# Float64 weight decode inside an attention and MLP kernel: one 4 KB row per partition and weight piece, the integer add on VectorE, words in a contiguous tile

## The chip, the core and the metric

The kernel runs on one core of a Trainium2 chip. The metric is device time in microseconds (us), the median of several executions. A core has a matrix engine (TensorE, PE in the profile; its weight loads are PEld), three elementwise engines (VectorE is DVE, ScalarE is ACT, GpSimd is POOL), and SyncE (SP), on whose queue all transfers of this kernel are issued. Each engine runs its own instructions in the order in which they stand; engines wait for each other on semaphores.

## The reference

Attention with a local window, a few global keys and a distance penalty, and behind it an MLP with GELU:

```python
scores = q @ k.T / 8                       # 4 batches, 8 heads, 768 tokens, head size 64
keep   = (col < n_global) | ((0 <= row - col) & (row - col < n_local))
dist   = n_local where only global, else abs(row - col)
a      = softmax(where(keep, scores - slope[h] * dist, -1e9))
x      = (a @ v)                           # 3072 tokens x 512
out    = gelu(x @ w_in) @ w_out            # w_in 512 x 2048, w_out 2048 x 512
```

`q`, `k` and `v` are float32. The two weight arrays arrive as float64, 8 MB each, and the kernel must make float32 numbers of them on the chip.

## The kernel before, in words

**The main loop.** The 3072 tokens are 12 chunks of 256, the 2048 columns of the hidden layer 8 slices of 256. Step T = 8 * chunk + slice, from 0 to 95, multiplies one chunk with one slice. `m1` (L457) makes the hidden values: 24 TensorE products named h (L468), 12 for each half of the slice, since each float32 operand is split in a high and a low part and three of the four products are taken. `gelu` (L472) applies GELU on ScalarE into gr (L478), makes its high part gh on GpSimd (L145) and its low part gl = gr - gh on VectorE (L148). `m2` (L483) multiplies gh and gl with the slice of `w_out` into acc (L495), 12 products. So TensorE needs gl of each step. gl0 is the low part of step 0, gl7 that of step 7: after it each slice has been used once. Steps -11 to -1 start the attention of chunks 0 and 1, whose scores and products run on float32 operands that are not split; its results go through xs (L422), a transpose (L452), xh (L454) and xl (L148) to become x. The attention of the later chunks is spread over the steps of the chunks before them (reductions n at L348, q at L277, k and others through L148).

**The weights.** A slice is four pieces of 512 KB, 128 partitions x 512 numbers x 8 bytes; I number them 4 * slice + i, from 0 to 31. Pieces i = 0 and 1 are 256 rows of `w_in` by the slice's 256 columns, which makes two runs of 2 KB per partition; i = 2 and 3 are 128 rows of `w_out`, 4 KB per partition. A piece lies in SBUF as pairs of 32-bit words, low and high word of a float64 side by side. The decode (L170 to L200) takes, per piece: on ScalarE, the low word times 2^-29, rounded to an integer, back into the low word's place (the scale, L184); on VectorE, 27 bits of the high word shifted by 3 (the mask, L186), into a contiguous tile `wb`; on GpSimd, the integer add of the two (the add, L188), into `wb`; on VectorE, that with the top two bits of the high word (the merge, L189), back into the high word's place, every second word; on ScalarE, a copy rounded to fp32r, the high part of the weight (the copy, L198); on VectorE, the difference, the low part (L200). fp32r is the float32 form that TensorE takes as a split operand. For pieces 12 and 26 GpSimd makes the high part instead, for piece 7 the low part (L42, L195, L199).

**Buffers.** Pieces of slices 0 to 6 rotate through five buffers (`ws`), those of slice 7 through the four of `stg`, which serve other loads too. A buffer is free again when its last reader is done: before, the low part of L200, since the finished float32 lies in it. Transfers of pieces are kept in order. From step 16 to 48 each piece is loaded once more, and three ScalarE operations check that its exponents lie in the range in which the short decode is right (`check_words`, L205); their scratch tile comes from `stg`.

**The order.** The program is written step by step: slice s is decoded at step `DECODE[s]` (L39: -4, -3, -2, -1, 0, 2, 2, 2), ahead of that step's other work. But the order in which instructions stand on each engine is not the written one: a scheduler arranges them by its own model of costs and by the dependencies, and it runs anew for the changed kernel.

Of the kernel before, what the change touches and what calls it, by code (L numbers as in the profile page):

```python
# [28 lines left out]
MAXLOCAL = 97.0  # L29
# chunks whose attention runs in native float32 products; the others split their operands  # L30
NATIVE = (0, 1)
# step at which a chunk's attention starts, and the steps after it at which its parts are issued
START = [-10, -5, 4] + [8 * c - 13 for c in range(3, NCH)]
# [3 lines left out]
       "pt": (2, 3, 4, 5), "av": (2, 3, 4, 5), "xt": (3, 4, 5, 6)}  # L37
# step at which a weight slice is decoded; slices from LATE on live where the native chunks' operands were
DECODE = (-4, -3, -2, -1, 0, 2, 2, 2)  # L39
LATE = 5  # L40
# work that GpSimd takes over from the other engines: weight halves (high, low part), V of a chunk
HI_POOL, LO_POOL, V_POOL = (12, 26), (7,), (2,)  # L42
NEGMASK = -1000000000.0
# [22 lines left out]
class Fast:  # L66
    def __init__(self, tc, ctx, qT, kT, v, w_in, w_out, out, limits):
        self.tc, self.nc = tc, tc.nc
        self.qT, self.kT, self.v, self.w_in, self.w_out, self.out = qT, kT, v, w_in, w_out, out
# [79 lines left out]

    def word_src(self, s, i):  # L150
        if i < 2:
            return self.w_in[i * 256:(i + 1) * 256, s * 512:(s + 1) * 512].rearrange("(d p) f -> p d f", p=P)
        r = s * 256 + (i - 2) * P
        return self.w_out[r:r + P, :].rearrange("p (d f) -> p d f", d=2)

    def load_words(self, s, i, use):
        pool, tag = (self.ws, "ws") if use == "w" and s < NST - 1 else (self.stg, "stage")
        w = pool.tile([P, 2, 256, 2], I32, name=f"{use}{s}_{i}", tag=tag)
        ins = self.nc.sync.dma_start(w.rearrange("p d f t -> p d (f t)"), self.word_src(s, i)).ins
# [10 lines left out]
    def split_weights(self, s):  # L170
# [9 lines left out]
        for i in range(4):  # L180
            w = self.raw.pop((s, i, "w"))
            lw, hw = w[:, :, :, 0], w[:, :, :, 1]
            a, t = hw, lw
            nc.scalar.activation(out=t, in_=lw.bitcast(U32), func=AF.Copy, scale=2.0 ** -29)  # L184
            bt = self.sm.tile([P, 2, 256], I32, name=f"wb{s}_{i}", tag="o")
            nc.vector.tensor_scalar(out=bt, in0=hw, scalar1=0x07FFFFFF, scalar2=3,  # L186
                                    op0=ALU.bitwise_and, op1=ALU.logical_shift_left)
            nc.gpsimd.tensor_tensor(out=bt, in0=bt, in1=t, op=ALU.add)  # L188
            nc.vector.scalar_tensor_tensor(out=a, in0=hw, scalar=-0x40000000, in1=bt,  # L189
                                           op0=ALU.bitwise_and, op1=ALU.bitwise_or)  # L190
            if i < 2:
                hi, lo = (x[:, 2 * i:2 * i + 2, :] for x in self.win[s])
            else:
                hi, lo = (x[:, i - 2, :].rearrange("p (d f) -> p d f", d=2) for x in self.wout[s])
            if s * 4 + i in HI_POOL:  # L195
                self.hi_pool(hi, a.bitcast(F32))
            else:
                nc.scalar.copy(hi, a.bitcast(F32))  # L198
            eng = nc.gpsimd if s * 4 + i in LO_POOL else nc.vector  # L199
            eng.tensor_tensor(out=lo, in0=a.bitcast(F32), in1=hi.bitcast(F32), op=ALU.subtract)  # L200

# [400 lines left out]
def round_words(nc, pool, out, src):  # L602
    n = out.shape[1]
# [3 lines left out]
    nc.sync.dma_start(w.rearrange("p f t -> p (f t)"), src)  # L607
    lw, hw = w[:, :, 0], w[:, :, 1]
# [29 lines left out]

def general(tc, qT, kT, v, w_in, w_out, out, limits):
    nc = tc.nc  # L640
    NB = S // P
    NF = DF // P
    with ExitStack() as ctx:
# [92 lines left out]

def body(tc, qT, kT, v, w_in, w_out, limits, out):
    nc = tc.nc
    w_in, w_out = w_in.bitcast(I32), w_out.bitcast(I32)
    with tc.tile_pool(name="flagp", bufs=1) as fp:  # L740
        flag_i = fp.tile([1, 1], I32, name="flag_i")
        with ExitStack() as ctx:
            fast = Fast(tc, ctx, qT, kT, v, w_in, w_out, out, limits)
            fast.run()
            fast.flag(flag_i)
        fv = nc.values_load(flag_i, min_val=0, max_val=1)
        with tc.If(fv):
            general(tc, qT, kT, v, w_in, w_out, out, limits)

# [21 lines left out]
```

## Time and profile before

| what | value |
|---|---|
| median of 3 runs | 737.23 us (736.77 to 737.34) |
| span of the profiled execution | 735.9 us |
| TensorE busy | 709.4 us, 96% of the span |
| VectorE, ScalarE, GpSimd busy | 481.6, 420.9, 349.4 us |
| mean granted TensorE clock | 0.994 |
| masks of the decode (L186), first and last start | 12.0 and 120.1 us |
| low part of step 0 and of step 7 (gl0, gl7), start | 71.35 and 127.82 us |

One execution was profiled, and all durations come from it. A row of a timeline is: start in us, duration in us, engine, line, operation, output<-inputs, size, and in square brackets how long the engine had been idle before and what ended that. A row of groups is: line, engine, operation and tiles, count, then busy us, mean ns of one, then idle us before them. The duration of one instruction holds its start-up and its tail, and consecutive ones overlap a little, so that the distance of two starts can be less than the duration of the first. A row with x2 in a timeline stands for two instructions in succession. Line numbers are those of the kernel before.

### The profile page before, as it was taken

Reading aid. Unit: us, or ns where it says so; the run is one execution under the profiler, and the core shown is the slowest. Engines: PE = TensorE matmul, PEld = TensorE weight load, DVE = VectorE, ACT = ScalarE, POOL = GpSimd, SP = SyncE. Lnnn points to the kernel's source line nnn. Section 1 sums busy time; section 2 is a strip of 40 time slices with the busy share of each in tenths; the row PEclk is TensorE's granted clock in tenths of the full one; section 3 lists DMA queues with packets and bytes.
Section 4 is the critical chain, followed back from the end, with each engine's and each line's share of the span. In section 5 each row is a group of like instructions: output and inputs, shape, how many; then the busy total and the mean of one; then the engine's idle time right before and its main releaser. Section 6 shows DMA issues by size and latency. Waiting matters only on the chain.

```text
span 735.9 us, 13621 instructions
## 1 busy us (share of the span) xinstructions
PE 709.4 (96%) x4617; PEld 642.8 (87%) x4617; DVE 481.6 (65%) x1219; ACT 420.9 (57%) x1032; POOL 349.4 (47%) x607
## 2 busy tenths in 40 slices
PE   6899878999999999999999999999999999999996
PEld 4778667899999999999999999999999999999995
DVE  6989999757846856746756757757657758643111
ACT  5658544555759769769669556355355455452101
POOL 4666666674445555543444545543444545431110
PEclk9999999999999999999999999999999999999999
DMA  8964563333526546535546513223213211100000
GB/s 264 263 191 143 175 213 81 117 83 101 146 78 171 166 123 177 158 108 158 160 125 174 153 44 87 72 62 94 76 47 109 83 29 44 45 15 1 29 1 33
DMA packets 78492, 80.92 MB, mean 110 GB/s; under 512 B 12368, under 2 KB 63056, under 8 KB 78416
## 3 DMA queue, kind: packets, MB, share of 16 engines
q1 hardware_dynamic: 78416, 79.98, 37.5%
q8 instruction: 38, 0.62, 0.4%
q14 instruction: 38, 0.31, 0.1%
HBM read 73.66 MB, written 6.29 MB: 109 GB/s over the span
## 4 chain that ended last, share of the span: by engine, by line
PE 85%; DVE 8%; DMA 2%; issue 1%; ACT 1%; SPq 1%; POOL 1%; POOLq 0%; DVEq 0%; ACTq 0%
PE h L468 35%; PE acc L495 33%; PE t L389 5%; PE s L343 5%; PE av L431 5%; DMA w<-w_in 2%; DVE winl L200 2%; DVE w L189 2%; PE s L339 2%; DVE woutl L200 1%; DVE wb L186 1%; PE av L417 1%; DVE gl L148 1%; ACT n L363 0%; DVE n L348 0%
## 5 line engine op out<-in xcount | busy, mean ns | idle before, releaser
L468 PE MATMUL h<-xh,winh 128*128 128x256 f32 x768 | 221.1, 289 | 1.5 <-ACT xh L454 1.4
L468 PE MATMUL h<-xh,winl 128*128 128x256 f32 x768 | 218.6, 285 | 0.4 <-DVE winl L200 0.4
L468 PE MATMUL h<-xl,winh 128*128 128x256 f32 x768 | 218.9, 285 | 0.0
L495 PE MATMUL acc<-wouth,gl 128*128 128x512 f32 x384 | 150.0, 399 | 7.2 <-DVE gl L148 7.2
L495 PE MATMUL acc<-wouth,gh 128*128 128x512 f32 x384 | 154.4, 402 | 0.9 <-POOL gh L145 0.9
L468 PEld LDWEIGHTS h<-xh,winh 128*128 128x128 f32 x768 | 146.9, 192 | 7.2 <-ACT xh L454 1.8
L495 PE MATMUL acc<-woutl,gh 128*128 128x512 f32 x384 | 152.4, 397 | 0.0
L468 PEld LDWEIGHTS h<-xl,winh 128*128 128x128 f32 x768 | 147.2, 192 | 3.7 <-issue 0.3
L148 DVE TENSOR_TENSOR gl<-gr,gh 128x512 fp32r<-128x512 f32 x96 | 68.2, 710 | 122.9 <-POOL gh L145 122.3
L468 PEld LDWEIGHTS h<-xh,winl 128*128 128x128 f32 x768 | 147.3, 192 | 0.8 <-DVE winl L200 0.6
L478 ACT ACTIVATE gr<-h 128x512 f32<-128x512 f32 x96 | 57.3, 597 | 82.9 <-PE h L468 75.0
L376 POOL TENSOR_SCALAR n<-n,su 128x256 f32<-128x256 f32 (+1 forms) x160 | 71.2, 466 | 55.2 <-DVE su L368 37.5
L145 POOL TENSOR_SCALAR gh<-gr 128x512 fp32r<-128x512 f32 x96 | 64.0, 667 | 69.6 <-ACT gr L478 69.6
L363 ACT ACTIVATE n<-n,mn 128x256 f32<-128x256 f32 (+1 forms) x192 | 91.8, 480 | 8.3 <-DVE mn L348 8.0
L145 POOL TENSOR_SCALAR vt<-vr 128x256 fp32r<-128x256 f32 (+1 forms) x80 | 34.1, 426 | 130.8 <-PE av L431 83.6
L495 PEld LDWEIGHTS acc<-wouth,gl 128*128 128x128 f32 x384 | 72.8, 190 | 24.4 <-DVE gl L148 9.0
L495 PEld LDWEIGHTS acc<-wouth,gh 128*128 128x128 f32 x384 | 73.2, 191 | 12.3 <-POOL gh L145 1.3
L495 PEld LDWEIGHTS acc<-woutl,gh 128*128 128x128 f32 x384 | 73.2, 190 | 11.8
L348 DVE CUSTOM_DVE_ANT_0 n<-s,pen 128x256 f32<-128x256 f32 (+1 forms) x192 | 69.3, 394 | 16.1 <-PE s L343 13.6
L396 ACT CAST pt<-t 128x512 fp32r<-128x512 f32 (+1 forms) x80 | 44.3, 553 | 60.6 <-PE t L389 56.2
L438 ACT COPY t<-av 64x256 f32<-64x256 f32 x80 | 29.3, 367 | 83.0 <-PE av L431 79.9
L188 POOL TENSOR_TENSOR wb<-wb,w 128x512 int32<-128x512 int32 x32 | 48.0, 1501 | 36.6 <-DVE wb L186 17.3
(92 smaller groups left out, 1158.2 us busy)
## 6 DMA issues: line engine op xcount, KB each, us to landing
kr<-kT SPq DMA_DIRECT2D x112, 112.0 KB, 2.8
qr<-qT SPq DMA_DIRECT2D x88, 128.0 KB, 2.9
w<-w_in SPq DMA_DIRECT2D x16, 512.0 KB, 4.7
w<-w_out SPq DMA_DIRECT2D x16, 512.0 KB, 4.5
c<-w_in SPq DMA_DIRECT2D x16, 512.0 KB, 4.2
c<-w_out SPq DMA_DIRECT2D x16, 512.0 KB, 4.4
vr<-v SPq DMA_DIRECT2D x48, 128.0 KB, 2.3
out<-o SPq DMA_DIRECT2D x24, 256.0 KB, 2.1
```

What stands on the lines that cost most here:

```text
L145: self.nc.gpsimd.tensor_scalar(out=out, in0=in_, scalar1=scale, scalar2=0.0, op0=ALU.mult, op1=ALU.add)
L148: self.nc.vector.tensor_tensor(out=out, in0=in_, in1=hi.bitcast(F32), op=ALU.subtract)
L188: nc.gpsimd.tensor_tensor(out=bt, in0=bt, in1=t, op=ALU.add)
L343: nc.tensor.matmul(sp[:, j, :w], lhsT=qq[:, hh, j * P:(j + 1) * P], rhs=kt[:, t, 0 if first else j, :w], start=t == 0, stop=t == 1)
L348: nc.vector.tensor_tensor_reduce(out=nn[:, j, :w], in0=sp[:, j, :w], in1=pen, scale=-slope(h), scalar=3e38, op0=ALU.add, op1=ALU.min, accu ...
L363: ins = nc.scalar.activation(out=nn[:, j, :w], in_=nn[:, j, :w], func=AF.Exp, bias=mn[:, i:i + 1], scale=-1.0, accum_out=su[:, i:i + 1])
L376: nc.gpsimd.tensor_scalar(out=nn[:, j, :w], in0=nn[:, j, :w], scalar1=su[:, i:i + 1], scalar2=0.0, op0=ALU.mult, op1=ALU.add)
L389: nc.tensor.transpose(tp[:, i, :], nn[:, j, a * P:(a + 1) * P], self.ident)
L396: nc.scalar.copy(pt[:, :, 0, :], tp[:, :n, :])
L468: nc.tensor.matmul(hp[:, f, :], lhsT=w[:, d, f * P:(f + 1) * P], rhs=x[:, d, :], start=n == 0, stop=n == 3 * NP - 1)
L478: self.table(nc.scalar.activation(out=gr, in_=hp, func=AF.Gelu))
L495: nc.tensor.matmul(acc, lhsT=g[:, f, ks], rhs=w[:, f, :], start=s == 0 and n == 0, stop=s == NST - 1 and n == 5)
```

## The change

All weights become one array of 32 pieces, [32, 128, 512] of 8-byte numbers, laid out on the host so that each piece is one 4 KB row per partition. So pieces 0 and 1 of a slice, too, are one run per partition instead of two; bytes and transfers are as many as before. In the decode the two steps on the words change places, and all of mask, merge and add work in the contiguous tile `a` (named wb), the add on VectorE instead of GpSimd. Then the copy and the low part read `a`, and the last reader of a piece's buffer is the add. `a` has two buffers, of the pool that `wb` had. No piece's high or low part goes to GpSimd any more. The check's scratch tile `cq` comes from that same pool instead of `stg`. The general version behind a flag (`general`, `round_words`), which does not run on these inputs, reads the new array.

```diff
-HI_POOL, LO_POOL, V_POOL = (12, 26), (7,), (2,)
+V_POOL = (2,)
...
     def load_words(self, s, i, use):
         pool, tag = (self.ws, "ws") if use == "w" and s < NST - 1 else (self.stg, "stage")
-        w = pool.tile([P, 2, 256, 2], I32, name=f"{use}{s}_{i}", tag=tag)
-        ins = self.nc.sync.dma_start(w.rearrange("p d f t -> p d (f t)"), self.word_src(s, i)).ins
+        w = pool.tile([P, 512, 2], I32, name=f"{use}{s}_{i}", tag=tag)
+        ins = self.nc.sync.dma_start(w.rearrange("p f t -> p (f t)"), self.w[s * 4 + i]).ins
...
             w = self.raw.pop((s, i, "w"))
-            lw, hw = w[:, :, :, 0], w[:, :, :, 1]
-            a, t = hw, lw
-            nc.scalar.activation(out=t, in_=lw.bitcast(U32), func=AF.Copy, scale=2.0 ** -29)
-            bt = self.sm.tile([P, 2, 256], I32, name=f"wb{s}_{i}", tag="o")
-            nc.vector.tensor_scalar(out=bt, in0=hw, scalar1=0x07FFFFFF, scalar2=3,
+            lw, hw = w[:, :, 0], w[:, :, 1]
+            nc.scalar.activation(out=lw, in_=lw.bitcast(U32), func=AF.Copy, scale=2.0 ** -29)
+            a = self.sm.tile([P, 512], I32, name=f"wb{s}_{i}", tag="o")
+            nc.vector.tensor_scalar(out=a, in0=hw, scalar1=0x07FFFFFF, scalar2=3,
                                     op0=ALU.bitwise_and, op1=ALU.logical_shift_left)
-            nc.gpsimd.tensor_tensor(out=bt, in0=bt, in1=t, op=ALU.add)
-            nc.vector.scalar_tensor_tensor(out=a, in0=hw, scalar=-0x40000000, in1=bt,
+            nc.vector.scalar_tensor_tensor(out=a, in0=hw, scalar=-0x40000000, in1=a,
                                            op0=ALU.bitwise_and, op1=ALU.bitwise_or)
+            nc.vector.tensor_tensor(out=a, in0=a, in1=lw, op=ALU.add)
+            af = a.bitcast(F32)
...
-            if s * 4 + i in HI_POOL:
-                self.hi_pool(hi, a.bitcast(F32))
-            else:
-                nc.scalar.copy(hi, a.bitcast(F32))
-            eng = nc.gpsimd if s * 4 + i in LO_POOL else nc.vector
-            eng.tensor_tensor(out=lo, in0=a.bitcast(F32), in1=hi.bitcast(F32), op=ALU.subtract)
+            nc.scalar.copy(hi, af)
+            self.lo_dve(lo, af, hi)
...
-        q = self.stg.tile([P, 2, 256], F32, name=f"cq{n}", tag="stage", padded_shape=[P, 4, 256])
-        nc.scalar.activation(out=q, in_=w[:, :, :, 1], func=AF.Square, scale=2.0 ** -27)
+        q = self.sm.tile([P, 512], F32, name=f"cq{n}", tag="o")
+        nc.scalar.activation(out=q, in_=w[:, :, 1], func=AF.Square, scale=2.0 ** -27)
...
+    wi = np.ascontiguousarray(moe_w_in).view(np.int64).reshape(2, 2, P, NST, 256).transpose(3, 0, 2, 1, 4)
+    wo = np.ascontiguousarray(moe_w_out).view(np.int64).reshape(NST, 2, P, DM)
+    w = np.concatenate([wi.reshape(NST, 2, P, DM), wo], axis=1).reshape(NST * 4, P, DM)
```

**VectorE around the low part of step 0.** The scheduler also moves work. In the names below, `w3_2` is piece 2 of slice 3, and the last number is a buffer's. Before:

```order
L186 TENSOR_SCALAR wb3_2_734<-w3_2_237 128x512
L422 TENSOR_TENSOR xs1_1_713<-av1_1_679,su1_1_510 128x2x2x64
L366 TENSOR_TENSOR nmax_123<-nmax_123,mn1_3_664 128x4
L200 TENSOR_TENSOR winl3_716<-w3_0_233,winh3_715 128x512
L186 TENSOR_SCALAR wb3_3_741<-w3_3_239 128x512
L367 TENSOR_SCALAR su1_3_665<-su1_3_665 128x4
L189 SCALAR_TENSOR_TENSOR w3_2_237<-w3_2_237,wb3_2_734 128x512
L368 RECIPROCAL su1_3_665<-su1_3_665 128x4
L200 TENSOR_TENSOR winl3_716<-w3_1_235,winh3_715 128x512
L148 TENSOR_TENSOR gl0_780<-gr0_781,gh0_779 128x512
```

The same place in the changed program, with its own line numbers (L179 is the mask, L181 the merge, L183 the add, L148 the low part and gl):

```order
L148 TENSOR_TENSOR winl2_626<-wb2_1_637,winh2_625 128x512
L183 ISA wb2_2_644<-w2_2_193,wb2_2_644 128x1024
L148 TENSOR_TENSOR xl1_603<-xt1_0_690,xh1_602 128x256
L412 TENSOR_TENSOR xs1_1_713<-av1_1_679,su1_1_510 128x2x2x64
L356 TENSOR_TENSOR nmax_123<-nmax_123,mn1_3_664 128x4
L179 TENSOR_SCALAR wb2_3_651<-w2_3_195 128x512
L357 TENSOR_SCALAR su1_3_665<-su1_3_665 128x4
L148 TENSOR_TENSOR gl0_780<-gr0_781,gh0_779 128x512
L181 SCALAR_TENSOR_TENSOR wb2_3_651<-w2_3_195,wb2_3_651 128x512
L358 RECIPROCAL su1_3_665<-su1_3_665 128x4
```

Before, the 16th mask (slice 3, piece 3) stands ahead of gl0; now it is the 12th (slice 2, piece 3). The add is built as a custom instruction over 1024 half-words per partition.

**ScalarE, slices 5 and 6.** L184 is the scale and L198 the copy before; L177 and L189 are the same two in the changed program. Before:

```order
L184 ACTIVATE w5_2_253<-w5_2_253 128x512
L454 CAST xh1_602<-xt1_3_952 128x256
L198 CAST winh5_967<-w5_0_249 128x512
L478 ACTIVATE gr3_1102<-h3_1075 128x512
L184 ACTIVATE w5_3_255<-w5_3_255 128x512
L198 CAST winh5_967<-w5_1_251 128x512
```

Changed:

```order
L468 ACTIVATE gr4_1145<-h4_1118 128x512
L189 CAST wouth4_810<-wb4_3_834 128x512
L177 ACTIVATE w5_3_255<-w5_3_255 128x512
L177 ACTIVATE w6_0_257<-w6_0_257 128x512
L189 CAST winh5_967<-wb5_0_972 128x512
L189 CAST winh5_967<-wb5_1_979 128x512
```

Before, the copy of piece 20 (slice 5, piece 0) stands behind the scale of piece 22 (slice 5, piece 2); now it stands behind the scale of piece 24 (slice 6, piece 0).

**VectorE in the same slices, changed program:**

```order
L183 ISA wb5_0_972<-w5_0_249,wb5_0_972 128x1024
L179 TENSOR_SCALAR wb5_1_979<-w5_1_251 128x512
L181 SCALAR_TENSOR_TENSOR wb5_1_979<-w5_1_251,wb5_1_979 128x512
L148 TENSOR_TENSOR winl5_968<-wb5_0_972,winh5_967 128x512
L183 ISA wb5_1_979<-w5_1_251,wb5_1_979 128x1024
L179 TENSOR_SCALAR wb5_2_986<-w5_2_253 128x512
```

Mask and merge of a piece stand ahead of the low part of the piece before, and its add behind it; before, the mask was followed by work of other pieces while GpSimd added.

More of the change, by code (lines that the diff above doesn't have):

```diff
@@ L66, with __init__ @@
 class Fast:
-    def __init__(self, tc, ctx, qT, kT, v, w_in, w_out, out, limits):
+    def __init__(self, tc, ctx, qT, kT, v, w, out, limits):
         self.tc, self.nc = tc, tc.nc
-        self.qT, self.kT, self.v, self.w_in, self.w_out, self.out = qT, kT, v, w_in, w_out, out
+        self.qT, self.kT, self.v, self.w, self.out = qT, kT, v, w, out
         self.limits = limits
@@ L148, in lo_dve @@
         self.nc.vector.tensor_tensor(out=out, in0=in_, in1=hi.bitcast(F32), op=ALU.subtract)
[L150 to L154, printed above, removed]
     def load_words(self, s, i, use):
         pool, tag = (self.ws, "ws") if use == "w" and s < NST - 1 else (self.stg, "stage")
-        w = pool.tile([P, 2, 256, 2], I32, name=f"{use}{s}_{i}", tag=tag)
-        ins = self.nc.sync.dma_start(w.rearrange("p d f t -> p d (f t)"), self.word_src(s, i)).ins
+        w = pool.tile([P, 512, 2], I32, name=f"{use}{s}_{i}", tag=tag)
+        ins = self.nc.sync.dma_start(w.rearrange("p f t -> p (f t)"), self.w[s * 4 + i]).ins
         if use == "w":
@@ L181, in split_weights @@
             w = self.raw.pop((s, i, "w"))
[L182 to L186 removed]
+            lw, hw = w[:, :, 0], w[:, :, 1]
+            nc.scalar.activation(out=lw, in_=lw.bitcast(U32), func=AF.Copy, scale=2.0 ** -29)
+            a = self.sm.tile([P, 512], I32, name=f"wb{s}_{i}", tag="o")
+            nc.vector.tensor_scalar(out=a, in0=hw, scalar1=0x07FFFFFF, scalar2=3,
                                     op0=ALU.bitwise_and, op1=ALU.logical_shift_left)
[L188 to L189 removed]
+            nc.vector.scalar_tensor_tensor(out=a, in0=hw, scalar=-0x40000000, in1=a,
                                            op0=ALU.bitwise_and, op1=ALU.bitwise_or)
+            nc.vector.tensor_tensor(out=a, in0=a, in1=lw, op=ALU.add)
+            af = a.bitcast(F32)
             if i < 2:
[L192 removed]
+                hi, lo = (x[:, 2 * i:2 * i + 2, :].rearrange("p d f -> p (d f)") for x in self.win[s])
             else:
[L194 to L200 removed]
+                hi, lo = (x[:, i - 2, :] for x in self.wout[s])
+            nc.scalar.copy(hi, af)
+            self.lo_dve(lo, af, hi)
     def check_load(self, n):
@@ L602, in round_words @@
 def round_words(nc, pool, out, src):
-    n = out.shape[1]
+    n = 512
     ti = lambda name: pool.tile([P, n], I32, name=name)
@@ L606, in round_words @@
     w = pool.tile([P, n, 2], I32, name="r_w")
-    nc.sync.dma_start(w.rearrange("p f t -> p (f t)"), src)
+    for k, x in enumerate(src):
+        m = n // len(src)
+        nc.sync.dma_start(w[:, k * m:(k + 1) * m, :].rearrange("p f t -> p (f t)"), x)
     lw, hw = w[:, :, 0], w[:, :, 1]
@@ L636, in round_words, with general @@
     nc.vector.tensor_copy(out, m)
-def general(tc, qT, kT, v, w_in, w_out, out, limits):
+def general(tc, qT, kT, v, w, out, limits):
     nc = tc.nc
@@ L654, in general @@
                 for f in range(NP):
+                    cols = slice(d % 2 * 512, d % 2 * 512 + 512)
                     round_words(nc, rw, wi[:, d, f * 512:(f + 1) * 512],
-                                w_in[d * P:(d + 1) * P, f * 1024:(f + 1) * 1024])
+                                [w[(2 * f + k) * 4 + d // 2, :, cols] for k in range(2)])
             for f in range(NF):
-                round_words(nc, rw, wo[:, f, :], w_out[f * P:(f + 1) * P, :])
+                round_words(nc, rw, wo[:, f, :], [w[f // 2 * 4 + 2 + f % 2]])
         icol = cst.tile([P, S], I32, name="g_icol")
@@ L734, in general, with body @@
                 nc.sync.dma_start(out[bass.ds(b * S + i * P, P), :], o)
-def body(tc, qT, kT, v, w_in, w_out, limits, out):
+def body(tc, qT, kT, v, w, limits, out):
     nc = tc.nc
-    w_in, w_out = w_in.bitcast(I32), w_out.bitcast(I32)
+    w = w.bitcast(I32)
     with tc.tile_pool(name="flagp", bufs=1) as fp:
@@ L742, in body @@
         with ExitStack() as ctx:
-            fast = Fast(tc, ctx, qT, kT, v, w_in, w_out, out, limits)
+            fast = Fast(tc, ctx, qT, kT, v, w, out, limits)
             fast.run()
@@ L747, in body @@
         with tc.If(fv):
-            general(tc, qT, kT, v, w_in, w_out, out, limits)
+            general(tc, qT, kT, v, w, out, limits)
 def kernel(q, k, v, n_global, n_local, moe_w_in, moe_w_out):
@@ L760 @@
         "v": np.ascontiguousarray(v.transpose(0, 2, 1, 3)).reshape(B, S, DM),
-        "w_in": np.ascontiguousarray(moe_w_in).view(np.int64),
-        "w_out": np.ascontiguousarray(moe_w_out).view(np.int64),
+        "w": np.ascontiguousarray(w),
         "limits": np.array([n_local, n_global]),
```

## Prediction

> **What bounds the kernel now.** I read the page's busy shares and its 40 slices first, then the table of stretches, then TensorE's waits in the stretch that is not full.
>
> ```profile
> PE 709.4 (96%) x4617; PEld 642.8 (87%) x4617; DVE 481.6 (65%) x1219; ACT 420.9 (57%) x1032; POOL 349.4 (47%) x607
> DVE  6989999757846856746756757757657758643111
> ...
> 28.00:60.00 32.00, 32.00 (x140) 26.09 (x141) 28.73 (x68) 20.89 (x57) 21.42 (x23) 1.00 0.71 204
> 60.00:128.00 68.00, 56.17 (x343) 48.11 (x341) 67.71 (x102) 36.78 (x70) 42.18 (x35) 0.95 0.51 157
> ...
> 148.00:250.00 102.00, 102.00 (x704) 94.67 (x703) 68.43 (x191) 68.72 (x170) 52.86 (x106) 1.00 0.42 118
> ...
> PE acc L495 <- DVE gl L148: 7.2, 5, 2.3
> PE xt L452 <- DVE xs L422: 2.0, 1, 2.0
> ```
>
> In a stretch's row the busy times stand in the order PE, PEld, DVE, ACT, POOL, then the granted clock. From 148 us on TensorE is never idle, so nothing there can be won. From 28 to 60 it is full too, and VectorE has 3.3 us to spare. From 60 to 128 VectorE is full (67.71 of 68) and TensorE is idle for 11.8 us; 9.2 of these are waits for VectorE. So the change is decided between 60 and 128 us, where the decode runs on VectorE: whatever moves the last decode moves the end. One execution is profiled; its span is 735.9 us, 1.3 below the median of 737.2. I take these 1.3 for what lies around the span, and add all differences to 737.2.
>
> **What the removed GpSimd add costs.** It costs VectorE time, though it runs elsewhere:
>
> ```profile
> 81.26 0.41 DVE L186 TENSOR_SCALAR wb<-w 128x512 int32<-128x512 int32 x1
> 81.59 0.68 DVE L200 TENSOR_TENSOR winl<-w,winh 128x512 fp32r<-128x512 f32 x1
> 82.19 1.78 DVE L189 SCALAR_TENSOR_TENSOR w<-w,wb 128x512 int32<-128x512 int32 x1
> 83.90 0.41 DVE L148 TENSOR_TENSOR xl<-xt,xh 128x256 fp32r<-128x256 f32 x1
> ...
> 81.90 1.52 POOL L188 TENSOR_TENSOR wb<-wb,w 128x512 int32<-128x512 int32 x1 [1.12 <-DVE wb L186]
> ...
> L189 DVE SCALAR_TENSOR_TENSOR w<-w,wb 128x512 int32<-128x512 int32 x20 | 19.8, 990 | 0.0
> L200 DVE TENSOR_TENSOR winl<-w,winh 128x512 fp32r<-128x512 f32 x10 | 14.5, 1452 | 0.0
> L200 DVE TENSOR_TENSOR woutl<-w,wouth 128x512 fp32r<-128x512 f32 x12 | 14.2, 1181 | 0.1
> ```
>
> A two-input operation over 512 words takes 0.68 us and the next starts 0.60 after it; the mask of L186 takes 0.41 and spaces 0.33. The operation that meets the GpSimd add takes 1.78. The groups (60 to 128 us) give the total: 20 times 0.31, 10 times 0.77 and 12 times 0.50, together 19.9 us for 20 adds, about 1.0 each.
>
> **What the new add costs.** The trace of before has no such add. In the built program it is not a 512-word operation: its row says 128x1024, half-words. From below it costs what a two-input operation over 512 words spaces, 0.60; from above twice the streaming, 0.60 + 0.53 = 1.13 (the 512-word operation takes 0.27 us more than the 256-word one at 83.90, so 512 more elements take 0.53). I take 0.75: the row of 512 words is the nearer one, but one input is read in pairs at a stride. So per piece VectorE loses 1.0 and gains 0.75: nearly an exchange. The VectorE page of the Trainium skill (VectorE: DVE Perf Modes, Mode 2×_1P) lets two inputs of 16-bit elements at step 1 go two a cycle; by it the sum would use the lower end, and no row here shows such an operation. A rule that speaks against the change: the GPSIMD Engine Reference (Engine selection, the paragraph on exact integer add) says that GpSimd adds 32-bit words exactly and the ordinary elementwise path computes in fp32; the 1024 half-words of the built row agree, and by it the upper end would hold unless the first rule applies.
>
> **Contiguous words, DMA shape, the three GpSimd halves.** The strided L200 at 81.59 takes 0.68, as does the contiguous gl below, so contiguity buys nothing. Both shapes of a piece land alike:
>
> ```profile
> w<-w_in SPq DMA_DIRECT2D x16, 512.0 KB, 4.7
> w<-w_out SPq DMA_DIRECT2D x16, 512.0 KB, 4.5
> c<-w_in SPq DMA_DIRECT2D x16, 512.0 KB, 4.2
> c<-w_out SPq DMA_DIRECT2D x16, 512.0 KB, 4.4
> ```
>
> The w_out pieces already are 4 KB rows: 0.2 less in one pair, 0.2 more in the other, so 0. Two high halves come to ScalarE (0.66 each, half idle there) and one low half to VectorE (0.60, before the first gl). The check's scratch tile leaves the stage buffers; from 148 us TensorE is full, so 0 there, and if that cover failed the waits would show in that stretch.
>
> **The order, and the sum.** The decode and gl (the low part of a GELU, on which TensorE waits) share VectorE's queue. Before, 16 masks stand ahead of the first gl; now 12. Four more pieces must pass between gl0 and gl7.
>
> ```profile
> 68.13 0.62 POOL L145 TENSOR_SCALAR gh<-gr 128x512 fp32r<-128x512 f32 x1 [0.41 <-ACT gr L478]
> 71.35 0.68 DVE L148 TENSOR_TENSOR gl<-gr,gh 128x512 fp32r<-128x512 f32 x1
> 93.47 0.84 DVE L186 TENSOR_SCALAR wb<-w 128x512 int32<-128x512 int32 x1
> 110.42 0.41 DVE L348 CUSTOM_DVE_ANT_0 n<-s,pen 128x256 f32<-128x256 f32 x1
> 110.76 0.08 DVE L348 DVE_READ_ACCUMULATOR2_ANT mn<- 128x1 f32 x1
> 116.58 0.76 DVE L277 SCALAR_TENSOR_TENSOR q<-qr,q 64x256 fp32r<-64x256 f32 x2
> 125.97 1.92 DVE L148 TENSOR_TENSOR k<-kr,k 128x448 fp32r<-128x448 f32 x2
> 127.82 1.04 DVE L148 TENSOR_TENSOR gl<-gr,gh 128x512 fp32r<-128x512 f32 x1
> 140.22 0.61 DVE L148 TENSOR_TENSOR k<-kr,k 128x448 fp32r<-128x448 f32 x1
> ```
>
> (1) gl0 started at 71.35, though its gh was ready at 68.75. With four pieces fewer ahead it can start at 68.75. Not earlier: its GELU hangs on TensorE, full from 28 to 60.
>
> (2) From gl0 to gl7 the new VectorE order holds 20 masks (0.335 each, 6.7), 21 merges (12.6), 22 low parts (13.2), 21 adds (15.8) and other work: 7 gl (4.2), 5 of xl and xs (0.34, 1.7), 8 reductions n (0.34, 2.7), 4 q (0.38, 1.5), 4 k (about 0.53, 2.1). Together 60.5.
>
> (3) gh still collides: the mask at 93.47 took 0.84 for 0.41. Seven times 0.43 is 3.0.
>
> (4) A new wait. A piece's buffer is freed by its add, and there are five buffers; ScalarE, in order, now has the scale of piece j+4 ahead of the copy of piece j (before, of j+2).
>
> ```profile
> 78.14 3.65 SPq L159 DMA_DIRECT2D w<-w_in  x2
> ...
> 82.49 0.67 ACT L184 ACTIVATE w<-w 128x512 int32<-128x512 uint32 x1 [1.68 <-DMA w<-w_in]
> ...
> 84.01 0.66 ACT L198 CAST wouth<-w 128x512 fp32r<-128x512 f32 x1 [0.59 <-DVE w L189]
> ```
>
> From issue (78.14) to the scale (82.49) 4.35 us pass; with scale and copy, 5.6. Between the add of piece j-1, which frees the buffer, and the low part of j VectorE has only mask, merge, low part, add, mask, merge: 3.2 us, 3.8 with a gl. So up to 2 us of wait at each of five such places (pieces 12, 14, 15, 17, 20), and all the decode behind waits; other work covers some, so I take 5 for the five together, between 0 and 10.
>
> gl7 then comes at 68.75 + 60.5 + 3.0 + 5 = 137.2, against 127.82: 9.4 later.
>
> (5) TensorE's order has 24 more h products ahead of gl7's last use than before:
>
> ```profile
> 81.02 0.28 PE L468 MATMUL h<-xl,winh 128*128 128x256 f32 x1
> 81.14 0.28 PE L468 MATMUL h<-xh,winl 128*128 128x256 f32 x1
> ```
>
> They start 0.12 apart, so 2.9 us less are left. Sum: +6.5, that is 743.7; I say **743**, since 5 for the copies is the softest term.
>
> **Rivals.**
> *The exchange is a gain.* The add at 0.60 (-3.2), no copy waits (-5): +6.5 turns into -1.7, 735.5. The short idle times may go too:
>
> ```profile
> 84.70 0.44 PE L452 MATMUL xt<-ident,xs 128*128 128x128 f32 x2 [1.96 <-DVE xs L422]
> ...
> 87.00:89.00 2.00, 1.65 (x5) 0.86 (x4) 2.00 (x5) 0.92 (x2) 0.54 (x1) 0.50 0.44 43
> ```
>
> After an idle time of 1.96 us TensorE ran at a granted clock of 0.50 for some 3.4 us; two such spells (the other at 107) cost at most 3.4 together. So 732 to 735.5, say 734. For it: VectorE's excess of 1.0 per add is real. Against: the decode starts four pieces behind. The page TensorE: Matmul & The Clock Gate (Part 1: The HAM clock gate) has the clock fall only after an idle window of about 3.4 us; this trace disagrees, 1.96 sufficed, and by that rule this rival would end at 735.5.
> *The terms cancel.* Add at 0.60 to 0.75, copies held little: -1.7 + 2.5 at the one end, +6.5 - 5 at the other: +0.8 to +1.5, say 738.
> *The add runs at double length.* 21 times 0.38 more is +8.0; VectorE is then slower than the buffers, so (4) falls to nothing: +9.5, 747; with (4) kept, 751.5. Say 749. Against: the row it is nearest to.
> *Fewer, larger packets speed the start.* The rows above allow 0.2 us a piece; five pieces stand before TensorE's first h: under 1 us.
>
> **How the numbers follow.** What a measurement of this kernel can tell from no change is about 0.2%, 1.5 us. Forecast (743, own range 739 to 747): 0.46, all slower. The gain (734): 0.25, faster. Cancelling (738): 0.17, of which 0.16 within 0.2%, 0.01 faster. Double length (749): 0.12, slower. That is 0.26, 0.16, 0.58. The range leaves out 0.1 at either end: from the middle of the gain, 733, to the double add, 749.
>
> **What would show it.** The add's own row: 0.68 to 0.83 us long (0.75 spacing), or 1.2. The first gl near 68.8 and the eighth near 137; if the eighth comes before 130, the gain is right. VectorE idle before low parts, released by ScalarE's copies, some 5 us in all: term (4); none: it falls. No 1.78 us merges left. TensorE's wait for gl well above 7.2 us. Idle TensorE behind 148 us, or a first gl before 67 or after 71, would make the frame of the sum wrong.

## The result, and the profile after

The changed kernel takes 749.07 us in the median of 4 runs (743.86 to 755.73); the kernel before took 737.29 beside it (736.77 to 737.81). The ratio is 1.0139, with a 95% interval of 1.0100 to 1.0179: slower, by about 1.4%. Medians here are over all executions; ratios leave out those that took over 1.5% longer than the fastest of the same kernel (one of the four here, three of twelve with the scratch undone, three of eight with the check loaded earlier), so the two need not agree. The profiled execution has a span of 747.0 us, 11.1 more than before. All differences below are between these two executions, unless an experiment is named.

Where did the 11 us go? The first view is the table of stretches, of the changed kernel:

```profile
28.00:60.00 32.00, 31.05 (x160) 25.82 (x159) 25.15 (x76) 19.20 (x54) 8.41 (x14) 0.79 0.72 199
60.00:128.00 68.00, 56.26 (x337) 48.46 (x337) 63.47 (x127) 36.56 (x68) 10.10 (x15) 0.92 0.54 167
...
148.00:200.00 52.00, 52.00 (x357) 47.93 (x356) 37.05 (x102) 32.20 (x78) 28.61 (x59) 1.00 0.39 109
200.00:400.00 200.00, 193.21 (x1284) 175.77 (x1283) 123.27 (x332) 148.00 (x364) 90.60 (x178) 0.99 0.53 144
400.00:730.00 330.00, 330.00 (x2229) 304.35 (x2228) 190.01 (x499) 151.14 (x384) 137.59 (x262) 1.00 0.20 58
```

and its one row of the kernel before that the prediction does not show:

```profile
200.00:400.00 200.00, 200.00 (x1361) 184.86 (x1360) 130.35 (x353) 155.57 (x377) 95.64 (x186) 1.00 0.52 147
```

Between 60 and 128 us, where the prediction put the whole matter, TensorE is as busy as before (56.26 against 56.17). Between 200 and 400 us it was never idle before; now it is idle for 6.8 us and runs 77 products fewer. That is where the check of the exponents runs (steps 16 to 48).

The second view is the start of gl, step by step, read from VectorE's timeline in both kernels. It dates the loss:

| step | before, us | after, us | difference |
|---|---|---|---|
| 0 | 71.35 | 63.86 | -7.49 |
| 7 | 127.82 | 130.21 | +2.39 |
| 12 | 164.53 | 164.04 | -0.49 |
| 24 | 243.43 | 244.76 | +1.33 |
| 26 | 258.67 | 267.74 | +9.07 |
| 34 | 314.81 | 327.35 | +12.54 |
| 52 | 438.48 | 449.40 | +10.92 |
| 95 | 725.60 | 736.52 | +10.92 |

At step 12, five steps after each slice has been used once, the changed kernel is half a microsecond ahead. From step 52 to the end the difference stays between 10.58 and 10.93. All of the loss lies between steps 12 and 52, and 7.7 us of it between steps 24 and 26, though single steps go up and down by a few us. The timeline of these two steps, changed kernel, transfers of check pieces (c) on SP first, then the engines:

```profile
254.74 0.54 SPq L153 DMA_DIRECT2D c<-w  x1
...
263.89 0.66 ACT L199 ACTIVATE cq<-c 128x512 f32<-128x512 int32 x1 [3.13 <-DMA c<-w]
264.58 0.36 ACT L428 COPY t<-av 64x256 f32<-64x256 f32 x1
264.97 0.60 ACT L468 ACTIVATE gr<-h 128x512 f32<-128x512 f32 x1
...
266.00 0.40 POOL L145 TENSOR_SCALAR vt<-vr 128x256 fp32r<-128x256 f32 x1 [3.82 <-DMA vr<-v]
266.36 0.62 POOL L145 TENSOR_SCALAR gh<-gr 128x512 fp32r<-128x512 f32 x1
...
267.04 0.50 PE L485 MATMUL acc<-wouth,gh 128*128 128x512 f32 x1 [2.96 <-POOL gh L145]
267.37 0.40 PE L485 MATMUL acc<-woutl,gh 128*128 128x512 f32 x1
268.49 0.79 PE L485 MATMUL acc<-wouth,gl 128*128 128x512 f32 x1 [0.72 <-DVE gl L148]
269.08 0.63 PE L485 MATMUL acc<-wouth,gh 128*128 128x512 f32 x1
269.51 0.63 PE L485 MATMUL acc<-woutl,gh 128*128 128x512 f32 x1
```

ScalarE stands idle for 3.13 us until a check piece has landed, 9.1 us after its transfer was issued. The check is needed by nobody until the very end, but the copy t and the GELU of a step stand behind it in ScalarE's order. GpSimd makes gh only after the GELU and after vt, which waited 3.82 us for a transfer of V; TensorE waits 2.96 us for gh. The two waits end almost together: the GELU is done at 265.57, and vt could start at 266.00. So this row alone does not show that the check costs anything: without ScalarE's wait gh would still have stood behind vt. Both wait for transfers that land late here: the check piece took 9.1 us from issue to landing (the median of the check pieces is 4.4), the first of these pieces of V 5.9 (2.4). After the idle time the products of 512 columns start 0.43 us apart instead of 0.23; TensorE's granted clock is 0.50 from 268.5 to 271.9 us.

Late landing is common in this stretch. Of the 202 transfers issued between the gl of step 12 and that of step 52, 31 took more than 5 us to land; before it were 7 of 198.

The waits from 150 to 440 us, changed kernel (us in total, times, longest):

```profile
POOL gh L145 <- ACT gr L468: 30.6, 15, 3.8
...
ACT cq L199 <- DMA c<-w: 11.1, 8, 3.1
```

and before:

```profile
POOL gh L145 <- ACT gr L478: 10.8, 9, 2.1
...
ACT cq L209 <- DMA c<-w_in: 1.6, 4, 0.4
```

### The profile page after: what moved, and what is told of

It reads as the page before. It is cut to its first block, busy times and chain, and to the rows that moved or that the text cites. A ratio compares the mean times of both kernels' runs of the same rounds, so it can differ in the third digit from the quotient of the medians.

```text
span 747.0 us, 13543 instructions
## 1 busy us (share of the span) xinstructions
PE 712.5 (95%) x4617; PEld 643.3 (86%) x4617; DVE 474.8 (64%) x1252; ACT 418.9 (56%) x1034; POOL 295.0 (39%) x572
## 4 chain that ended last, share of the span: by engine, by line
PE 73%; DMA 9%; ACT 8%; DVE 6%; issue 3%; SPq 1%; POOL 1%; POOLq 0%; ACTq 0%; DVEq 0%
PE h L458 30%; PE acc L485 28%; PE t L379 4%; PE s L333 4%; PE av L421 4%; DMA w<-w 4%; DMA c<-w 3%; ACT n L353 2%; DMA kr<-kT 1%; PE s L329 1%; DVE wb L183 1%; PE av L407 1%; ACT gr L468 1%; ACT cq L200 1%; ACT cq L199 1%
## 5 line engine op out<-in xcount | busy, mean ns | idle before, releaser
L485 PE MATMUL acc<-wouth,gh 128*128 128x512 f32 x384 | 156.1, 407 | 10.4 <-POOL gh L145 10.2
L148 DVE TENSOR_TENSOR gl<-gr,gh 128x512 fp32r<-128x512 f32 x96 | 68.6, 715 | 120.1 <-POOL gh L145 119.7
L145 POOL TENSOR_SCALAR k<-kr 128x448 fp32r<-128x448 f32 (+1 forms) x80 | 45.8, 574 | 43.0 <-PE s L333 21.3
```

Of the source, the lines that this page charges most:

```text
L145: self.nc.gpsimd.tensor_scalar(out=out, in0=in_, scalar1=scale, scalar2=0.0, op0=ALU.mult, op1=ALU.add)
L148: self.nc.vector.tensor_tensor(out=out, in0=in_, in1=hi.bitcast(F32), op=ALU.subtract)
L485: nc.tensor.matmul(acc, lhsT=g[:, f, ks], rhs=w[:, f, :], start=s == 0 and n == 0, stop=s == NST - 1 and n == 5)
```

## The experiments

The theory after the profile (A): the loss is made by one line of the change, the check's scratch tile that moved from the stage buffers to the pool of the output tiles. Its rivals: the 4 KB rows land later (B), or the new decode pushes attention work into the check (C). Where nothing else is said, a diff is against the changed kernel.

**One part undone: the scratch.**

```diff
-        q = self.sm.tile([P, 512], F32, name=f"cq{n}", tag="o")
+        q = self.stg.tile([P, 512], F32, name=f"cq{n}", tag="stage", padded_shape=[P, 1024])
```

> The changed kernel with one part undone: the check's scratch tile comes from the stage buffers again, as in the kernel before. Theory A (the loss is made in the check, because its scratch shares two buffers with the output tiles and frees a stage buffer for another early load): the time falls to 738 to 740, ScalarE no longer waits 3 us for a piece of the check, and TensorE is not idle from 200 to 400 us. Theory B (the 4 KB rows land later beside other loads) and theory C (the new decode shifts the attention work into the check): 746 to 750, with TensorE still idle for several us between 200 and 400.

Measured: 738.09 us (733.76 to 745.52, 12 runs), ratio 1.0015 (0.9991 to 1.0038). TensorE between 200 and 400 us:

```profile
200.00:400.00 200.00, 200.00 (x1361) 184.76 (x1360) 135.28 (x362) 157.06 (x383) 98.55 (x190) 1.00 0.52 150
```

The loss is gone, with the whole decode and all transfers of the change in place. ScalarE no longer shows a wait for a check piece, and 2 transfers instead of 31 take more than 5 us to land.

**One part alone: the scratch, in the kernel before.**

```diff
-        q = self.stg.tile([P, 2, 256], F32, name=f"cq{n}", tag="stage", padded_shape=[P, 4, 256])
+        q = self.sm.tile([P, 2, 256], F32, name=f"cq{n}", tag="o")
```

> The kernel before with one part of the change done: the check's scratch tile comes from the pool of the output tiles. Decode and transfers stay as before. Theory A: 744 to 748, with ScalarE waiting for pieces of the check and TensorE idle for 5 us or more between 200 and 400 us. Theories B and C: 736 to 738.

Measured: 747.63 us (744.05 to 750.71, 6 runs), ratio 1.0132 (1.0104 to 1.0161). This one line makes the whole loss. A holds from both sides; C falls.

**One part undone: the transfers.** Two runs of 2 KB for the pieces of `w_in`; no engine's order differs, only the sources on SP.

```diff
-        w = pool.tile([P, 512, 2], I32, name=f"{use}{s}_{i}", tag=tag)
-        ins = self.nc.sync.dma_start(w.rearrange("p f t -> p (f t)"), self.w[s * 4 + i]).ins
+        w = pool.tile([P, 2, 256, 2], I32, name=f"{use}{s}_{i}", tag=tag)
+        ins = self.nc.sync.dma_start(w.rearrange("p d f t -> p d (f t)"), self.word_src(s, i)).ins
```

> The changed kernel with the transfers of before: pieces of w_in as two runs of 2 KB per partition again. The order on all engines is that of the changed kernel. Theory A: no difference from the changed kernel, 744 to 750. Theory B: 738 to 741.

Measured: 748.34 us (743.71 to 750.30, 4 runs), ratio 1.0129 (1.0096 to 1.0162). No difference from the changed kernel; B falls.

**One part undone: the add's engine.**

```diff
-            nc.vector.tensor_tensor(out=a, in0=a, in1=lw, op=ALU.add)
+            nc.gpsimd.tensor_tensor(out=a, in0=a, in1=lw, op=ALU.add)
```

> The changed kernel with the add on GpSimd again (still behind the merge, in the contiguous tile). The prediction's price says that VectorE pays about 1.0 us for each GpSimd add that meets it and 0.60 (measured) for its own: low parts or merges of 1.1 to 1.8 us come back, the eighth gl starts 4 to 8 us later than in the changed kernel (130.2), and the time is 752 to 757. If the exchange is worth nothing, the eighth gl is within 2 us of 130.2 and the time is that of the changed kernel.

Measured: 751.40 us (749.88 to 752.80, 4 runs), ratio 1.0198 (1.0175 to 1.0221), against 1.0139 (1.0100 to 1.0179) for the changed kernel: 2 to 4 us slower, at the edge of what the runs tell. The eighth gl starts at 132.22, 2.0 later than in the changed kernel, at the edge between the two expectations; but in the profile of the two runs of 2 KB, whose engines have the changed kernel's order, it starts at 134.49, so 2 us tell nothing here. The collisions themselves are back, on other operations than before. VectorE's groups between 60 and 128 us (busy us, mean ns) with the add on GpSimd:

```profile
L179 DVE TENSOR_SCALAR wb<-w 128x512 int32<-128x512 int32 x20 | 21.5, 1073 | 0.4
...
L148 DVE TENSOR_TENSOR gl<-gr,gh 128x512 fp32r<-128x512 f32 x7 | 8.2, 1178 | 1.0 <-POOL gh L145 1.0
```

and in the changed kernel:

```profile
L183 DVE CUSTOM_DVE_ANT_0 wb<-w,wb 128x1024 uint16<-128x1024 uint16 x22 | 16.3, 740 | 0.1
L181 DVE SCALAR_TENSOR_TENSOR wb<-w,wb 128x512 int32<-128x512 int32 x21 | 14.9, 707 | 0.4
L179 DVE TENSOR_SCALAR wb<-w 128x512 int32<-128x512 int32 x21 | 9.4, 447 | 0.0
...
L148 DVE TENSOR_TENSOR gl<-gr,gh 128x512 fp32r<-128x512 f32 x7 | 4.8, 682 | 1.8 <-POOL gh L145 1.8
```

Twenty masks cost 12 us more and seven gl 3.4 more when GpSimd adds, so the price per add is real; the end hardly feels it.

**One part alone: the add's engine, in the kernel before.**

```diff
-            nc.gpsimd.tensor_tensor(out=bt, in0=bt, in1=t, op=ALU.add)
+            nc.vector.tensor_tensor(out=bt, in0=bt, in1=t, op=ALU.add)
```

> The kernel before with one part of the change done: the add of the decode on VectorE (ahead of the merge, in the same tiles); layout, merge, check, GpSimd's three halves as before. By the prediction's prices VectorE loses about 1.0 us per add to GpSimd and pays 0.60 itself, so 20 adds save 8 us of VectorE between 60 and 128 us, the eighth gl comes up to 8 us earlier (127.8 before) and the time is 729 to 734. If the exchange is worth nothing because other waits bind: 736 to 738.

Measured: 737.08 us (732.61 to 739.41, 10 runs), ratio 1.0002 (0.9985 to 1.0019). The stretches:

```profile
28.00:60.00 32.00, 29.62 (x119) 23.25 (x118) 25.26 (x69) 17.50 (x47) 10.21 (x14) 0.63 0.71 203
60.00:128.00 68.00, 59.70 (x378) 52.91 (x378) 62.25 (x131) 38.48 (x72) 14.41 (x16) 0.95 0.52 162
```

VectorE has 5.5 us less to do between 60 and 128 (62.25 against 67.71) and TensorE 3.5 us more; yet the eighth gl starts at 127.92, 0.10 later than before, and the time does not change. What replaced VectorE as the limit is in TensorE's waits of the whole execution:

```profile
PE s L339 <- POOL qr L145: 5.1, 2, 4.0
PE acc L495 <- POOL gh L145: 4.6, 2, 3.2
PE h L468 <- ACT gr L478: 2.7, 2, 1.7
PE av L417 <- ACT pt L392: 2.0, 2, 1.7
PE h L468 <- ACT xh L454: 1.9, 1, 1.9
PE acc L495 <- DVE gl L148: 1.5, 1, 1.5
```

The first of these is there before too (5.3 us). The 7.2 us of waits for gl are 1.5 now; waits for gh and waits that lead to ScalarE have taken their place. ScalarE in turn stood before scales of pieces that had not landed (19.0 us in 18 waits from 28 to 150 us, 11.2 in 10 before). One thing weakens the reading of this profile: its execution had TensorE at half clock for 24 us (last section). The times of the others, at a mean clock of 0.992 to 0.999, speak for the same, but what they waited for was not profiled.

**The three halves on GpSimd**, taken away from that kernel:

```diff
-HI_POOL, LO_POOL, V_POOL = (12, 26), (7,), (2,)
+HI_POOL, LO_POOL, V_POOL = (), (), (2,)
```

> The kernel before, with the add on VectorE and none of the three halves on GpSimd (two copies more on ScalarE, one low part more on VectorE); layout, merge and check as before. If GpSimd's two copies of high parts, for which it waited 20 us with gh behind them, held the add alone back: 731 to 735. If the decode's transfers and ScalarE's waits bind in any case: 736 to 738.

Measured: 743.19 us (734.77 to 745.41, 10 runs), ratio 1.0069 (1.0033 to 1.0104). The expectation had the sign wrong: in this decode the three halves are worth 5 us by the ratios, 6 by the medians (eight executions took 741 to 745 us, two 735).

Both undone parts together, scratch and halves, in the changed kernel:

```diff
-V_POOL = (2,)
+HI_POOL, LO_POOL, V_POOL = (12, 26), (7,), (2,)
...
-        q = self.sm.tile([P, 512], F32, name=f"cq{n}", tag="o")
+        q = self.stg.tile([P, 512], F32, name=f"cq{n}", tag="stage", padded_shape=[P, 1024])
...
-            nc.scalar.copy(hi, af)
-            self.lo_dve(lo, af, hi)
+            if s * 4 + i in HI_POOL:
+                self.hi_pool(hi, af)
+            else:
+                nc.scalar.copy(hi, af)
+            eng = nc.gpsimd if s * 4 + i in LO_POOL else nc.vector
+            eng.tensor_tensor(out=lo, in0=af, in1=hi.bitcast(F32), op=ALU.subtract)
```

> The changed kernel with two parts undone: the check's scratch comes from the stage buffers again, and GpSimd makes the high parts of pieces 12 and 26 and the low part of piece 7 again. Transfers, add on VectorE and contiguous tile stay. With the halves moved, the add alone on VectorE went from 737.1 to 743.2 us; if that holds in the new decode too, this kernel takes 731 to 735 and beats the one before. If the decode's order hides them: 737 to 739, as with the scratch alone undone.

Measured: 736.58 us (733.77 to 741.46, 12 runs), ratio 0.9987 (0.9965 to 1.0010). It does not beat the kernel before, and is 1.5 us from the kernel with the scratch alone undone, which the intervals do not tell apart. So what the halves are worth there does not carry over to the new decode.

**Why the scratch costs anything.** Two theories: the two buffers shared with the output tiles tie the checks to the chunks' ends and bunch them (A1); or a scratch in the stage buffers held things back in a useful way, and any other place loses that (A2).

Two buffers of its own, in space that is free after the decode:

```diff
+            self.cqp = self.ctx.enter_context(self.tc.tile_pool(name="cqp", bufs=2))
...
-        q = self.sm.tile([P, 512], F32, name=f"cq{n}", tag="o")
+        q = self.cqp.tile([P, 512], F32, name=f"cq{n}", tag="cq")
```

> The changed kernel, with two buffers for the check's scratch alone (in space that is free after the decode): it shares them neither with the output tiles nor with the stage buffers. Theory A1 (the two buffers shared with the output tiles tie the checks to the ends of the chunks and bunch them): 736 to 740, the checks spread over the chunks as in the kernel before. Theory A2 (the scratch, as long as it took stage buffers, held back loads; without it they come in bursts): 744 to 749, as in the changed kernel.

Measured: 753.43 us (752.48 to 760.66, 4 runs), ratio 1.0258 (1.0201 to 1.0314): slower still, and slower than either theory had it. And no scratch at all, where the piece keeps its stage buffer through all three operations of the check instead of one:

```diff
-        q = self.sm.tile([P, 512], F32, name=f"cq{n}", tag="o")
+        q = w[:, :, 0].bitcast(F32)
```

> The changed kernel, with the check's squares written over the low words of the piece itself, so that it needs no scratch at all. A1: 736 to 740. A2: 744 to 749.

Measured: 777.54 us (773.38 to 781.14, 4 runs), ratio 1.0537 (1.0503 to 1.0572). A1 falls: with buffers of its own nothing ties the checks to the output tiles, and it is worse. The time from the issue of a check piece's transfer to the square that reads it hints at why. Matched in order, its median is 11.5 us before, 7.2 in the changed kernel, and 4.1 with buffers of its own, where no piece has more than 7.7. My reading, argued and not shown: with the scratch in a stage buffer, a square can stand in ScalarE's order only when such a buffer is free, and by then its piece has mostly landed; elsewhere the scheduler puts it where it believes the piece to land, and ScalarE, in order, pays for each later landing. With the scratch alone moved the median is 7.3, as in the changed kernel. It does not order all kernels (without any scratch, the slowest, it is 4.7); the waits do better. Waits of ScalarE for check pieces from 150 to 440 us, with buffers of its own:

```profile
ACT cq L200 <- DMA c<-w: 29.9, 20, 5.1
```

**Loading earlier.** The check two steps behind its load, scratch as in the change:

```diff
-            if 17 <= T < 49:
-                self.check_words(T - 17)
+            if 18 <= T < 50:
+                self.check_words(T - 18)
```

> The changed kernel, scratch still in the output tiles' buffers, but each check piece is loaded two steps ahead of its use instead of one. If ScalarE's waits for landing pieces are what costs (11.1 us, with GELU behind them): they fall below 4 us and the time to 738 to 743. If the bunching alone costs, because ScalarE is filled: 745 to 750.

Measured: 744.22 us (735.17 to 751.38, 8 runs), ratio 1.0038 (1.0006 to 1.0070). ScalarE's waits for check pieces fall from 11.1 to 2.6 us, as expected, and the time by 5 us by the medians and 7 by the ratios, at the edge of the expected 743; the runs scatter widely. Now 43 transfers take more than 5 us to land.

The same edit with buffers of its own:

> The kernel with buffers of its own for the check's scratch (753.4 us), and each check piece loaded two steps ahead of its use instead of one. Theory L: the distance from a piece's transfer to its square, 4.3 us in the middle of the order, grows by up to a step (7 us), the waits of ScalarE for landing pieces fall from 24.8 us to under 8, and the time to 738 to 744. If the distance is not what counts: 750 to 756.

Measured: 751.80 us (750.46 to 753.81, 4 runs), ratio 1.0212 (1.0184 to 1.0239). The edit did not do what it was for: the scheduler gave all engines and the transfers the same order as without it, the median distance stayed at 4.1 us and the waits at 29.5. So this run tells nothing on the theory; it repeats the one with buffers of its own.

**Nothing to wait for.** Check pieces loaded and not read, squares on a tile that is there; the check is left out by its last constant:

```diff
-        nc.scalar.activation(out=q, in_=w[:, :, 1], func=AF.Square, scale=2.0 ** -27)
+        nc.scalar.activation(out=q, in_=self.win[0][0].rearrange("p d f -> p (d f)").bitcast(I32)[:, 0:1024:2],
+                             func=AF.Square, scale=2.0 ** -27)
...
-        nc.vector.memset(self.cbias[:, 1:2], -240.0)
+        nc.vector.memset(self.cbias[:, 1:2], -1e30)
```

> The changed kernel, with the check's squares read from a weight tile that has long been in SBUF, and the check's last constant set so that they flag nothing; the check pieces are still loaded, but nobody reads them. So this kernel leaves the check of the exponents out. The squares stand in the same bunches behind the output tiles. Theory L (ScalarE, in order, waits for check pieces that land late, with GELU behind): 736 to 740. Theory S (the bunches fill ScalarE): 745 to 749.

Measured: 743.22 us (741.96 to 750.95, 4 runs), ratio 1.0114 (1.0050 to 1.0178). By its time this is undecided: the median lies between the two expectations, and the interval reaches over both. In the profile 7.1 of the 11.4 us that the changed kernel loses between steps 12 and 52 stay. The edit also does more than it is for: the transfers stand in another order too, since pieces that nobody reads free their buffers earlier.

All profiles together, sorted by the waits; the loss is what the start of gl falls behind the kernel before between steps 12 and 52, so the decode is not in it:

| kernel | ScalarE's waits for check pieces, us | loss, us |
|---|---|---|
| scratch undone (e1) | none | 0.1 |
| add alone, scratch in stage (e9) | none | 0.1 |
| without halves, scratch in stage (e13) | 0.2 | 0.3 |
| scratch and halves undone (e14) | 0.2 | -0.7 |
| nothing to wait for (e10) | none | 7.1 |
| loaded earlier (e8) | 2.6 | 5.9 |
| scratch alone (e2) | 7.3 | 10.4 |
| two runs of 2 KB (e3) | 9.2 | 9.4 |
| add on GpSimd (e4) | 10.5 | 10.3 |
| the change | 11.1 | 11.4 |
| own buffers, earlier (e11) | 29.5 | 17.2 |
| own buffers (e6) | 29.9 | 17.1 |
| in place (e7) | 53.1 | 43.2 |

With the scratch in the stage buffers there is no loss, four times out of four. Elsewhere it grows with ScalarE's waits, but some 6 to 7 us stay when these are gone or nearly gone. The traces of those two kernels show what more than half of this is: waits for pieces of V. With nothing to wait for on ScalarE, at 180 us:

```profile
178.26 0.30 POOL L145 TENSOR_SCALAR vt<-vr 128x128 fp32r<-128x128 f32 x1 [4.04 <-DMA vr<-v]
178.59 0.29 DVE L306 TENSOR_TENSOR vt<-vr,vt 128x128 fp32r<-128x128 f32 x1 [3.38 <-POOL vt L145]
...
180.07 0.91 PE L379 MATMUL t<-ident,n 128*128 128x128 f32 x4 [2.09 <-DVE mn L338]
```

GpSimd waits for a piece of V, VectorE for GpSimd, and TensorE for the reduction mn that stands behind in VectorE's order. The 2.09 us of idle time, and the 1.7 us that TensorE then loses at a granted clock of 0.50 from 180.3 to 183.8, are 3.8 of the 7.1 us. Loaded earlier:

```profile
263.22 0.58 ACT L468 ACTIVATE gr<-h 128x512 f32<-128x512 f32 x1
...
267.63 0.41 POOL L145 TENSOR_SCALAR vt<-vr 128x256 fp32r<-128x256 f32 x1 [5.31 <-DMA vr<-v]
268.00 0.41 POOL L145 TENSOR_SCALAR xh<-t 128x256 fp32r<-128x256 f32 x1
268.37 0.79 POOL L145 TENSOR_SCALAR gh<-gr 128x512 fp32r<-128x512 f32 x1
...
269.21 0.50 PE L485 MATMUL acc<-wouth,gh 128*128 128x512 f32 x1 [1.80 <-POOL gh L145]
```

The GELU was done 4.6 us before gh; GpSimd stood before vt. A second wait of 1.85 us, at 382.70, is of the same kind, and the two are 3.7 of the 5.9 us. In this kernel these pieces of V were issued behind check pieces and pieces of k and q, and took 6.0 to 7.1 us to land; before, no piece of V took more than 3.5 in these steps. GpSimd's waits for V from 150 to 440 us are in total, with nothing to wait for on ScalarE:

```profile
POOL vt L145 <- DMA vr<-v: 45.2, 15, 6.2
```

and before:

```profile
POOL vt L145 <- DMA vr<-v: 24.7, 15, 3.3
```

So the loss of the change has two kinds of waits, ScalarE's for check pieces and GpSimd's for pieces of V, and where they end together, as at 266 us, neither is the price by itself. That moving the scratch brings both is shown; that it does so because another order bunches the transfers is how I read it, and no run moved V's transfers alone.

## Why the prediction was right and wrong

The direction was right, and the time came out at 749.07 against a forecast of 743, at the upper end of the stated range (749.0); by the ratio it is 747.5. The mechanism was wrong: of the forecast's 6.5 us almost nothing is in the result, and the result stands at a term that the sum had at 0. That the number came so near is luck.

**The step that failed** is the sentence on the check's scratch: "from 148 us TensorE is full, so 0 there". A full TensorE was taken for cover. The term measured 11.4 us in the profiles, or 1.3% with the scratch alone moved. As I read the traces, TensorE was full only because the order kept long waits for transfers, of check pieces on ScalarE and of V on GpSimd, from falling ahead of the GELU's parts; a change of buffers changed that order, and the cover went with it. Idle TensorE behind 148 us had been named as what would make the frame of the sum wrong, and that is what came.

**The frame itself**, that the time is decided between 60 and 128 us where VectorE is full, failed too. With the scratch undone, the whole decode change is worth 1.0015 (0.9991 to 1.0038), nothing that can be told. With the add alone, VectorE was relieved of 5.5 us and nothing came of it. My reading is that VectorE was one of several limits of about the same height. The rival in which the terms cancel (738) is how the decode came out.

**The removed add.** Its price was right: no operation of 1.78 us is left, and merges and low parts take 0.71 and 0.69 us in the mean between 60 and 128 us, against 0.99 and 1.18 to 1.45 before.

**The new add** takes 0.68 us and spaces 0.60, the lower bound; 0.75 was said. Rows of the changed kernel:

```profile
75.27 0.68 DVE L183 CUSTOM_DVE_ANT_0 wb<-w,wb 128x1024 uint16<-128x1024 uint16 x1
75.88 0.41 DVE L148 TENSOR_TENSOR xl<-xt,xh 128x256 fp32r<-128x256 f32 x1
...
115.21 1.09 DVE L183 CUSTOM_DVE_ANT_0 wb<-w,wb 128x1024 uint16<-128x1024 uint16 x1
```

1024 half-words take what 512 words take, also with one input in pairs at a stride, and the double-length rival is out. By the rule that the prediction named from the VectorE page of the Trainium skill (VectorE: DVE Perf Modes, Mode 2×_1P), two 16-bit inputs go two a cycle; this row agrees. The 0.15 put on top, 21 times or 3.2 us, was not there. (For this rival with the copy waits kept, the terms add up to 751.7, not 751.5; nothing hangs on it.)

**(1) The first gl** came at 63.86, not 68.75. "Not earlier" rested on TensorE being full from 28 to 60; but its order changed as well: in that stretch it did 160 products where it had done 140, at a mean granted clock of 0.79.

**(2) and (3)** From the first to the eighth gl it took 66.4 us; 60.5 + 3.0 + 5 = 68.5 was said. The collisions with gh are there (the add at 115.21 took 1.09; six operations of the decode in that time took 0.2 to 0.43 too long, about 2.3 in all against 3.0).

**(4) The copy waits** were 1.6 us, not 5: four times VectorE was idle before a low part until ScalarE's copy, between 0.22 and 0.80. The buffers' loop hardly stopped VectorE. ScalarE waited longer at scales of pieces still to land, but most of that wait was there before. Waits of the changed kernel from 60 to 130 us:

```profile
ACT w L177 <- DMA w<-w: 13.6, 15, 1.6
...
PE acc L485 <- POOL gh L145: 6.6, 3, 2.8
```

and of the kernel before:

```profile
ACT w L184 <- DMA w<-w_out: 5.6, 5, 2.1
ACT w L184 <- DMA w<-w_in: 5.6, 5, 1.9
```

So 13.6 us stand against 11.2. TensorE no longer waited for gl (7.2 us before) but for gh, 6.6 us, which follows the GELU on ScalarE. "TensorE's wait for gl well above 7.2" was the wrong wait.

**(5)** The eighth gl came 2.39 late, not 9.4. That 2.9 us less were then left fits: at step 12 the difference is -0.49. One profile is not exact to a few us here: with the transfers of before and the same order on all engines, the eighth gl was 6.67 late and step 12 3.97.

**At nothing** were also the three halves. In the new decode 1.5 us, not told from nothing; in the old one, without its GpSimd adds, 5 to 6 us. And the DMA shape, rightly: 749.07 and 748.34.

## What to carry to other kernels

A full engine in the profile is no cover for a change of buffers under a scheduler: what fills it is the order, and a tile pool is a part of what makes the order. Before work that nobody waits for is moved, look at what stands behind it on its in-order engine, and behind its transfers on their queue, and ask how long before its use each transfer is issued; a buffer that seems to hold such work back may be what gives the transfers their time. When a wait seems to name its cause, look whether a second one ends at the same moment. And a resource that is 99% busy in a stretch is a price only if the other limits lie lower: relieve it alone, in the kernel before, to see what comes next.

## What the runs showed of the hardware

TensorE's granted clock stayed at half for 24 us after a short idle time, with TensorE busy by its records all the while. In the kernel before with the add alone on VectorE, it was idle for 1.92 us before this product:

```profile
33.52 0.50 PE L468 MATMUL h<-xh,winh 128*128 128x256 f32 x2 [1.92 <-ACT xh L454]
```

and these are its stretches behind (busy PE, PEld, DVE, ACT, POOL, then the clock):

```profile
36.00:38.00 2.00, 2.00 (x6) 1.39 (x6) 1.64 (x6) 0.94 (x2) 0.35 (x1) 0.50 0.97 268
...
56.00:58.00 2.00, 2.00 (x12) 2.00 (x11) 2.00 (x8) 1.09 (x4) 0.00 (x0) 0.50 0.00 0
58.00:60.00 2.00, 2.00 (x17) 2.00 (x17) 0.68 (x3) 0.33 (x1) 0.00 (x0) 0.84 0.50 129
```

From 34.7 to 58.6 us, some 24 us, it ran at 0.50, without idle time by these rows. Spells at half clock last whole multiples of 3.41 us in this trace and in the two main ones: one in each spell of the kernel before (from 85.7 and from 106.2 us), four in the changed kernel's from 39.8 to 53.4, seven here. The page TensorE: Matmul & The Clock Gate of the Trainium skill (Part 1: The HAM clock gate) has the clock return after about 3.4 us of sustained work; here it took seven times that. Even so this kernel's time was that of the kernel before, and executions of it at a mean clock of 0.995 took no less (736.8 to 739.4 us): in that stretch, it seems, something else was the limit.
